# Issuing the later loads of K, Q and V one query tile apart in a fused LSH-attention and MLP kernel

## The chip, the cores and the metric

The kernel runs on one core of a Trainium2 chip. The metric is the device time of one execution in microseconds (us). Engines are named as in the profile: PE (TensorE matmul), PEld (its weight load), DVE (VectorE), ACT (ScalarE), POOL (GpSimd), SP (SyncE, whose queue issues most DMAs here).

## The reference

Attention with a hash mask, then an MLP. B, H, S, D = 4, 8, 768, 64; the MLP goes from 512 to 2048 and back to 512.

```python
q_bits = (einsum('bhsd,dk->bhsk', q, proj) > 0); k_bits = the same of k      # 6 bits
mask = q_bucket[:, :, :, None] == k_bucket[:, :, None, :]
scores = where(mask, D**-0.5 * q @ k^T, -1e9)
attn = exp(scores - max); attn = attn / (sum(attn) + 1e-9)
x = (attn @ v), heads side by side                                            # 3072 x 512
h = x @ w_in; g = where(h > 0, h, exp(min(h, 0)) - 1); out = g @ w_out
```

Everything is fp32 at the reference's precision; the kernel gets it from fp16 matmuls on numbers that are split into a high and a low half.

## The kernel before

**Tiling.** Heads go in pairs, four a batch. A chunk is half a batch's sequence (three columns of 128 rows) for all four pairs. The kernel walks through 8 chunks x 4 pairs x 6 query tiles = 192 query tiles; `G` counts them, and a batch has 48. For one tile, `scores` makes a 128 x 768 block in PSUM (`s` or `so`), DVE copies it with its maximum (`pt`), ACT takes the exponent, ACT and DVE split it into two fp16 halves (`hl`), and a DMA transpose on SP's queue turns it (`PT<-hl`). Four tiles after a pair's last query tile, `attend` multiplies `PT` by V (`av`), and `x<-av` copies the result out. In between, the matmuls of the MLP (`h`, `o`, and ACT's and DVE's work on `U`) of the chunk before are interleaved.

**Preparation.** Each pair needs Q per chunk, and K per batch. `prep_k` and `prep_q` have four steps: `load` (fp32 from HBM to `kst` and `qst`, two buffers each), `scale` (sums of squares on ACT, `natk,kx<-kst` and `nat1q,qx<-qst`, then powers of two on DVE), `split` (fp16 halves `natk`, `nat1q`, `nat2q`, then DMA transposes `K<-natk`, `O<-nat1q`, `O<-nat2q`), and `project` (DVE copies K, `COPY K<-K`; PE makes the hash bits `z`, DVE turns them into `zb`, small DMAs `K<-zb` and `O<-zb` put them under K and Q). `prep_v` loads V (`vf`, seven buffers shared with the split halves `vhl`), sums its squares (`natk,vx<-vf`) and splits it.

**What sets the order.** Pairs after the first four are prepared two at a time. The lists `due` and `vdue` hold each step with the query tile at which the code emits it. For a group whose first pair begins at tile `begin`, `lead` gives the tiles of loads and of sums: `begin` less `PREP[0]` and `PREP[1]`, but no earlier than the last split of the group before, which comes 16 tiles ahead of `begin`. V's steps stand at fixed tiles from the end of the batch before. From tile 30 on, PE follows the code's order. The other engines and SP's queue do not: a scheduler simulates the program and lets an instruction go ahead of earlier ones when its inputs and its buffers are free. Every queue is then strictly in order on the chip. SP's DMAs share eight semaphores in turn, so each also waits for the one eight issues ahead.

**What starts at the loads (before).** The tiles for batch 1's first K group were: all four loads (K, Q, K, Q) at 32, sums at 34, scales at 35, splits at 38 and 44. V's were: four loads at 32, sums at 34 to 37, scale at 41, splits at 43, 49, 54, 59.

Of the kernel before, what the change touches and what calls it, by code (L numbers as in the profile page):

```python
# [10 lines left out]
F32 = mybir.dt.float32  # L11
# [18 lines left out]
OTHER = (3, 3)  # L30
MOE_LAGS = (6, 6, 6)
AV_LAG = 4
PREP = (18, 14, 10, 5)
PREP0 = (100, 12, 12, 6)
W_RATE = 6
W_PRE = 2
# [5 lines left out]
V_AFTER = 0  # L42
W_FREE = 5
VPREP = (-50, 0, 1, 2, 4, 6)

# [19 lines left out]
def lsh_attention_moe(  # L67
# [10 lines left out]
    nc = tc.nc  # L78
    B, H, S, D = q.shape
# [3 lines left out]
    P = 128  # L83
    NC = S // P
    NP = H // 2
    HALF = S // 2
    HC = NC // 2
# [210 lines left out]
    kexs = {}  # L298

    def prep_k(b, ps, sts, sgs):  # L300
        def load():
            with after(0, "first") if b == 0 and "first" in ks[0, 0] else nullcontext():
                for p, st, sg_ in zip(ps, sts, sgs):
                    st["kf"] = stg.tile([P, 2 * NC, D], F32, tag="k", name="kst", bufs=2) if sg_.kf is None else sg_.kf
                    nc.sync.dma_start(
                        st["kf"].rearrange("p (h c) d -> p h (c d)", h=2),
                        k[b, 2 * p : 2 * p + 2].rearrange("h (p c) d -> p h (c d)", c=NC),
                    )

        def scale():  # L310
            w = len(ps)
            mx = small.tile([P, 2], F32, tag="kx", name="kx")[:, :w]
            for n, (st, sg_) in enumerate(zip(sts, sgs)):
                squares(mx[:, n : n + 1], flat(st["kf"]), sg_.k1)
            yield
            if b not in kexs:
                kexs[b] = small.tile([P, NP], F32, tag="ke", name="ke", bufs=2)
            _, sc = powers(mx, w, 4.0, QK_TOP, "k", squares=True, ex=kexs[b][:, ps[0] : ps[0] + w])
            for n, st in enumerate(sts):
                st["ksc"] = sc[:, n : n + 1]  # L320

        def split(st, sg_):
            s, nat = st["ksc"], sg_.k1
            scaled("n_hi", nat[:, :, :D], st["kf"], s)
            rest("n_lo", nat[:, :, D:], st["kf"], s, nat[:, :, :D])
            st["K1"] = okp.tile([P, 2 * NC, P], F16, tag="K1", name="K1", bufs=NP)
            st["K2"] = okp.tile([P, 2 * NC, P], F16, tag="K2", name="K2", bufs=NP)
            st["first"] = nc.sync.dma_start_transpose(st["K1"], flat(nat))

        def project(st):  # L330
            k1, k2 = flat(st["K1"]), flat(st["K2"])
            copied("dup", k2[:D], k1[:D])
            quads = [k1[:, u * HALF : (u + 1) * HALF] for u in range(4)]
            st["done"] = bits(k2, ((0, quads), (1, quads)), HALF, 0)

        return load, scale, split, project

    def prep_q(b, c0, nc_, ps, ksts, sts, sgs):
        def load():
            with after(0, "first") if b == 0 and "first" in ks[0, 0] else nullcontext():  # L340
                for p, st, sg_ in zip(ps, sts, sgs):
                    st["qf"] = stg.tile([P, 2 * HC, D], F32, tag="q", name="qst", bufs=2) if sg_.qf is None else sg_.qf
                    st["qf"] = st["qf"][:, : 2 * nc_, :]
                    nc.sync.dma_start(
                        st["qf"].rearrange("p (h c) d -> p h (c d)", h=2),
                        q[b, 2 * p : 2 * p + 2].rearrange("h (p c) d -> p h (c d)", c=NC)[:, :, c0 * D : (c0 + nc_) * D],
                    )

        def scale():
            w = len(ps)  # L350
            mx = small.tile([P, 2], F32, tag="qx", name="qx")[:, :w]
            for n, (st, sg_) in enumerate(zip(sts, sgs)):
                squares(mx[:, n : n + 1], flat(st["qf"]), sg_.q1[:, : 2 * nc_])
            yield
            ex, sc = powers(mx, w, 4.0, QK_TOP, "q", rows=True, squares=True)
            sg = small.tile([P, 2, 2], F32, tag="sg", name="sg")
            c = D**-0.5 * 2.0 ** (-2 * QK_TOP)
            for x in range(2):
                nc.vector.scalar_tensor_tensor(
                    sg[:, x, :w], ex, c if x == 0 else -c, kexs[b][:, ps[0] : ps[0] + w], ALU.mult, ALU.mult  # L360
                )
            for n, st in enumerate(sts):
                st["qsc"], st["sg"] = sc[:, n : n + 1], sg[:, :, n]

        def split(st, sg_):
            s, nat1, nat2 = st["qsc"], sg_.q1[:, : 2 * nc_, :], sg_.q2[:, : 2 * nc_, :]
            scaled("n_hi", nat1[:, :, :D], st["qf"], s)
            rest("n_lo", nat2[:, :, :D], st["qf"], s, nat1[:, :, :D])
            copied("dup", nat1[:, :, D:], nat1[:, :, :D])
            st["O1"], st["O2"] = o_ring.take(2 * nc_, (b, c0))  # L370
            nc.sync.dma_start_transpose(st["O1"], flat(nat1))
            nc.sync.dma_start_transpose(st["O2"], flat(nat2))

        def project(st):
            w = nc_ * P
            o1, o2 = flat(st["O1"]), flat(st["O2"])
            hi, lo = ([x[:, u * w : (u + 1) * w] for u in range(2)] for x in (o1, o2[:D]))
            st["made"] = bits(o2, ((2, hi), (2, lo), (3, lo)), w, 1)

        return load, scale, split, project  # L380


    def prep_v(b):
        st = {"f": [], "v": [None] * NP}

        def load():
            mx = small.tile([P, NP], F32, tag="vx", name="vx")
            for p in range(NP):
                f = vpool.tile([P, 2, NC, D], F32, tag="v", name="vf")
                with tc.issue_after(ks[b, V_AFTER]["done"].ins) if b == 0 else nullcontext():  # L390
                    nc.sync.dma_start(
                        f.rearrange("p h c d -> p h (c d)"),
                        v[b, 2 * p : 2 * p + 2].rearrange("h (p c) d -> p h (c d)", c=NC),
                    )
                st["f"].append(f)
            st["mx"] = mx
            if b == 0:
                for p in range(NP):
                    sums(p)

        def sums(p):
            f = st["f"][p]
            squares(st["mx"][:, p : p + 1], f.rearrange("p h c d -> p (h c d)"), steady.k1 if b else junk0)

        def top():
            m1 = small.tile([P, 1], F32, tag="vx1", name="vx1")
            with behind_max():
                nc.vector.tensor_reduce(m1, st["mx"], axis=AX.X, op=ALU.max)
            st["m1"] = m1

        def scale():
            with behind_max():
                st["ex"], st["sc"] = powers(st["m1"], 1, 2.0**-34, V_TOP, "v", squares=True)

        def split(p):
            f = st["f"][p]
            t = vpool.tile([P, 2, NC, 2, D], F16, tag="v", name="vhl")
            st["v"][p] = t
            for j in range(2):
                scaled("v_hi", t[:, j, :, 0, :], f[:, j], st["sc"])  # L420
                rest("v_lo", t[:, j, :, 1, :], f[:, j], st["sc"], t[:, j, :, 0, :])

        parts = [lambda p=p: sums(p) for p in range(NP)] if b else []
        return st, [load] + parts + ([top, scale] if b else [lambda: (top(), scale())]) + [lambda p=p: split(p) for p in range(NP)]


    wst = {}
# [284 lines left out]
    def prep(ns):  # L712
# [9 lines left out]
        if c["c0"] == 0:  # L722
            parts.insert(0, (prep_k(b, ps, ksts, sgs), ksts))

        def load():
            for part, _ in parts:
                part[0]()

        made = []

# [15 lines left out]
            part, sts = parts[x]  # L746
            part[3](sts[i])

        return load, sums, scale, split, project, len(parts)


    due = []
# [4 lines left out]
    for ns in groups:  # L757
# [18 lines left out]
            split_at[0] = max(lead[1], split_at[0])  # L776
        else:
            lead[0] = max(lead[0], last["split"])
            lead[1] = max(lead[1], lead[0])
            split_at[0] = max(split_at[0], lead[1], last["project"])  # L780
        steps = prep(ns)
        due += [(lead[0], ns[0], 0, steps[0]), (lead[1], ns[0], 1, steps[1]), (lead[1] + (not early), ns[0], 1.5, steps[2])]
        split_at[0] = max(split_at[0], due[-1][0])
        steps = steps[1:]
        for i, n in enumerate(ns):
# [15 lines left out]
        vs[b] = prep_v(b)  # L801
    for b in range(1, B):
        s0 = [c for c in chunks if c["b"] < b][-1]["end"]
        vdue += [(s0 + x, s) for x, s in zip((-16, -14, -13, -12, -11, -9, -7, -5, 1, 6, 11), vs[b][1])]


    wq = list(wsplits)
# [50 lines left out]
    def weights(n):  # L858
        nonlocal w_credit, w_at
        w_credit += n  # L860
        while w_credit >= 1:

            at = (w_at + (2 if w_at >= NSI else 1)) * SL
            users = {x[1] for x in due} | ({"v"} if len(vdue) == NP + 2 + (B - 1) * (2 * NP + 3) else set())
            if any(a < at + SL and at < z and users & u for a, z, u in guards):
                break
            if w_at not in w64 and w_at < NSI + NSO:
# [109 lines left out]
```

## Time and profile before

| | us |
|---|---|
| median of three runs | 940.16 (939.42 to 942.19) |
| the profiled execution | 942.09 |
| its span, first to last instruction | 940.3 |
| mean granted TensorE clock of the span | 0.955 |
| PE busy | 818.6 |
| DVE busy | 713.6 |
| ACT busy | 706.1 |

The time of an execution is a little longer than the span of its instructions. Rows of the profile below are in us from the span's start. A row of the timeline gives start, length, engine, source line, operation, output and inputs, shape and count; in brackets stands how long the engine was idle before it and what released it. `SPq` rows are DMA issues: their length is how long SP was held by the issue, and not how long the transfer took.

### The profile page before, as it was taken

What the parts mean: (1) busy time and instruction counts of PE and PEld (TensorE: products, weight loads), DVE (VectorE), ACT (ScalarE), POOL (GpSimd) and SP (SyncE); (2) the same over time, 40 slices, a digit from 0 to 9 for tenths busy, and PEclk for the clock granted to TensorE, in tenths of its full rate; (3) what the DMA queues carried; (4) which work ended last, traced back from release to release, by engine and by line L of the source; (5) the groups of instructions that cost most, each with busy time, mean ns of one, the idle gap of its engine ahead of it and who ended that gap; (6) DMA issues with size and microseconds to landing.
All of it is one profiled execution on the core that took longest, in us unless ns stands there. A gap on an engine that the chain in (4) does not pass through costs nothing.

```text
span 940.3 us, 14736 instructions
## 1 busy us (share of the span) xinstructions
PE 818.6 (87%) x4975; PEld 420.0 (45%) x4975; DVE 713.6 (76%) x1625; ACT 706.1 (75%) x1277; POOL 99.3 (11%) x142
## 2 busy tenths in 40 slices
PE   2446655899886999999987999999989999999997
PEld 0113222354443555554544554545545555555553
DVE  6799999898974878788974777788888687775332
ACT  4566786898967878878976877879887788786443
POOL 1000000011111010210010010210121102110000
PEclk9998665899998999999998999999999999999999
DMA  9999987679788767788698658787697767665000
GB/s 275 264 230 211 243 228 165 119 133 173 137 141 165 137 119 136 152 163 177 137 179 148 136 100 143 156 174 139 113 193 129 129 119 153 102 101 101 34 1 35
DMA packets 404924, 138.49 MB, mean 147 GB/s; under 512 B 380976, under 2 KB 399152, under 8 KB 404848
## 3 DMA queue, kind: packets, MB, share of 16 engines
q1 hardware_dynamic: 402864, 131.91, 70.8%
q0 software_dynamic: 1680, 5.51, 1.8%
q8 instruction: 39, 0.64, 0.3%
q14 instruction: 37, 0.30, 0.1%
q10 hardware_dynamic: 304, 0.13, 0.1%
HBM read 35.65 MB, written 6.29 MB: 45 GB/s over the span
## 4 chain that ended last, share of the span: by engine, by line
PE 46%; DVE 9%; ACT 5%; DMA 4%; issue 3%; POOL 1%; SPq 0%; DVEq 0%; ACTq 0%; POOLq 0%
PE o L646 16%; PE h L603 16%; PE s L508 6%; PE av L560 6%; DMA PT<-hl 3%; DVE pt L520 2%; DVE hl L152 2%; ACT pt L536 2%; DMA K<-natk 2%; POOL nb L533 1%; PE z L286 1%; DVE U L626 1%; ACT U L143 1%; ACT hl L143 1%; DVE vhl L152 1%
## 5 line engine op out<-in xcount | busy, mean ns | idle before, releaser
L646 PE MATMUL o<-W,U 128*128 128x512 f16 x1152 | 281.0, 381 | 2.8 <-ACT U L143 2.8
L603 PE MATMUL h<-x,W 128*128 128x384 f16 x1536 | 279.6, 326 | 0.8 <-DVE x L570 0.8
L536 ACT ACTIVATE pt<-pt,nb,sg 128x768 f32<-128x768 f32 x192 | 195.4, 1020 | 64.3 <-POOL nb L533 63.7
L152 DVE SCALAR_TENSOR_TENSOR hl<-pt,r,hl 128x768 f16<-128x768 f32 x192 | 190.7, 1011 | 11.5 <-ACT hl L143 11.4
L603 PEld LDWEIGHTS <-W 128*128 128x128 f16 x1536 | 147.5, 98 | 112.0 <-issue 10.9
L520 DVE TENSOR_SCALAR_CACHE_REDUCE pt<-s 128x768 f32<-128x768 f32 x177 | 168.1, 949 | 38.8 <-DMA PT<-hl 19.4
L143 ACT ACTIVATE hl<-pt,r 128x768 f16<-128x768 f32 x192 | 168.4, 925 | 16.0 <-issue 6.9
L508 PE MATMUL s<-K,O 128*128 128x384 f16 x708 | 153.6, 340 | 22.8 <-DVE pt L520 15.8
L646 PEld LDWEIGHTS <-U 128*128 128x128 f16 x1152 | 111.0, 98 | 124.6 <-issue 6.6
L533 POOL TENSOR_SCALAR nb<-m,sg 128x2 f32<-128x2 f32 x96 | 85.0, 886 | 746.8 <-DVE pt L520 392.5
L560 PE MATMUL av<-PT,vhl 128*64 128x384 f16 x1152 | 115.2, 353 | 24.9 <-DMA PT<-hl 22.3
L152 DVE SCALAR_TENSOR_TENSOR U<-U,sgg 128x384 f16<-128x384 f32 x128 | 78.6, 614 | 69.2 <-ACT U L143 68.3
L508 PEld LDWEIGHTS <-O 76*128 76x128 f16 (+1 forms) x768 | 74.5, 102 | 125.7 <-issue 50.7
L143 ACT ACTIVATE U<-U,sgg 128x384 f16<-128x384 f32 x128 | 77.8, 608 | 56.0 <-DVE U L626 55.8
L560 PEld LDWEIGHTS <-vhl 128*64 128x64 f16 x1152 | 72.3, 118 | 75.6 <-DMA PT<-hl 20.2
L626 DVE SCALAR_TENSOR_TENSOR U<-U 128x384 f32<-128x384 f32 x128 | 70.6, 552 | 37.0 <-ACT U L618 36.8
L616 ACT ACTIVATE U<-h,ch 128x384 f32<-128x384 f32 x128 | 72.6, 567 | 31.3 <-PE h L603 31.2
L618 ACT ACTIVATE U<-h,ch 128x384 f32<-128x384 f32 x128 | 72.8, 568 | 0.0
L472 PE MATMUL acc<-W,ones 128*128 128x512 bf16 x32 | 18.0, 562 | 40.1 <-DVE W L469 39.9
L536 ACT ACTIVATION_READ_ACCUMULATOR pt<-pt,nb,sg 128x1 f32 x192 | 36.3, 189 | 0.0
L570 DVE SCALAR_TENSOR_TENSOR x<-av,x 128x384 f16<-128x384 f32 x32 | 17.7, 554 | 19.3 <-ACT x L569 19.3
L291 DVE TENSOR_SCALAR zb<-z,pjt 64x384 f16<-64x384 f32 (+1 forms) x48 | 29.0, 603 | 0.3 <-PE z L286 0.3
(107 smaller groups left out, 520.5 us busy)
## 6 DMA issues: line engine op xcount, KB each, us to landing
U<-in_moe_w_in_dram SPq DMA_DIRECT2D x12, 512.0 KB
vf<-in_v_dram SPq DMA_DIRECT2D x16, 384.0 KB
U<-in_moe_w_out_dram SPq DMA_DIRECT2D x12, 512.0 KB
qst<-in_q_dram SPq DMA_DIRECT2D x30, 192.0 KB
kst<-in_k_dram SPq DMA_DIRECT2D x14, 384.0 KB
out_dram<-W POOLq DMA_DIRECT2D x14, 256.0 KB, 4.7
PT<-hl SPq DMA_TRANSPOSE x192
W<-in_moe_w_in_dram SPq DMA_DIRECT2D x4, 512.0 KB
```

Source lines behind the costliest of these rows:

```text
L143: nc.scalar.activation(o, x, AF.Copy, scale=s)
L152: nc.vector.scalar_tensor_tensor(o, x, s, hi, ALU.mult, ALU.subtract)
L508: nc.tensor.matmul(s_tile[:, n, :HALF], st[o][:rows, at, :], kst[kk][:rows, j * NC + n * HC : j * NC + (n + 1) * HC, :].rearrange("p a b - ...
L520: top = nc.vector.tensor_scalar(pt.rearrange("p (n e) -> p n e", n=2), s_tile[:, :, :HALF], CLAMP, None, ALU.max, ALU.max, accum_out=duo[0 ...
L533: nc.gpsimd.tensor_scalar(nb[:, :w], m[:, :w], st["sg"][:, 1:2], 1.0, ALU.mult, ALU.mult)
L536: nc.scalar.activation(pt, pt, AF.Exp, bias=nb[:, n : n + 1], scale=st["sg"][:, 0:1], accum_out=sm[:, n : n + 1])
L560: nc.tensor.matmul(av[j * D : (j + 1) * D], vt[:, j, c, vx, :], PTs[j][:, :, px, c, :], start=n == 0, stop=n == last,)
L603: nc.tensor.matmul(h, WH[:, g * KT + t, wx, fc * P : (fc + 1) * P], c["xs"][t][:, xx, :], start=n == 0, stop=n == 3 * KT - 1,)
L616: nc.scalar.activation(e, h, AF.Exp, scale=c["ch"])
L618: nc.scalar.activation(hp, h, AF.Relu, scale=c["ch"])
L626: nc.vector.scalar_tensor_tensor(e, e, -1.0, hp, ALU.add, ALU.min)
L646: nc.tensor.matmul(o[t][:, :DO], g16[:, gx, t * P : (t + 1) * P], WH[:, NSI + 1 + f, wx, :], start=f == 0 and i == 0, stop=f == NF - 1 and ...
```

## The change

`load` of K and Q now takes one pair at a time, `load` of V one pair of heads. In `due` each later group's loads stand one tile apart, from the tile at which all four stood (`PREP[0]` goes from 18 to 21, but the last split of the group before still decides), and the sums come at least three tiles after the first load. V's steps have 14 tiles of their own.

```diff
-PREP = (18, 14, 10, 5)
+PREP = (21, 14, 10, 5)
+VLATER = (-18, -17, -16, -14, -13, -12, -11, -10, -8, -6, -4, 1, 6, 11)
...
     def prep_k(b, ps, sts, sgs):
-        def load():
+        def load(i):
+            p, st, sg_ = ps[i], sts[i], sgs[i]
...
+        loads = [lambda part=part, i=i: part[0](i) for i in range(len(ns)) for part, _ in parts]
...
-            lead[1] = max(lead[1], lead[0])
+            lead[1] = max(lead[1], lead[0] + 3)
...
-        due += [(lead[0], ns[0], 0, steps[0]), (lead[1], ns[0], 1, steps[1]), (lead[1] + (not early), ns[0], 1.5, steps[2])]
+        if early:
+            due.append((lead[0], ns[0], 0, lambda loads=steps[0]: [load() for load in loads]))
+        else:
+            due += [(lead[0] + i, ns[0], 0, load) for i, load in enumerate(steps[0])]
+        due += [(lead[1], ns[0], 1, steps[1]), (lead[1] + (not early), ns[0], 1.5, steps[2])]
...
-        vdue += [(s0 + x, s) for x, s in zip((-16, -14, -13, -12, -11, -9, -7, -5, 1, 6, 11), vs[b][1])]
+        vdue += [(s0 + x, s) for x, s in zip(VLATER, vs[b][1])]
```

For batch 1's first K group this gives K at 32, Q at 33, K at 34, Q at 35, sums at 35, scales at 36, splits still at 38 and 44. V's loads stand at 30, 31, 32 and 34, its sums at 35 to 38, its scale at 42, its splits at 44, 49, 54 and 59.

What the scheduler makes of that is another matter. SP's queue in the middle of batch 2's first chunk (tiles 100 to 106), before; `K_4842<-zb` and `O_4848<-zb` are the copies of hash bits, `kst` holds K of the batch to come:

```order
190 L344 DMA qst<-in_q_dram 128x2x192 x2
191 L391 DMA vf<-in_v_dram 128x2x384
192 L305 DMA kst<-in_k_dram 128x2x384 x2
193 L552 DMA_TRANSPOSE PT<-hl 128x12x128 x2
194 L295 DMA K_4842<-zb 12x384 x4
195 L295 DMA O_4848<-zb 12x384 x2
196 L552 DMA_TRANSPOSE PT<-hl 128x12x128 x4
```

And the same place with the change:

```order
183 L345 DMA qst<-in_q_dram 128x2x192 x2
184 L392 DMA vf<-in_v_dram 128x2x384
185 L555 DMA_TRANSPOSE PT<-hl 128x12x128 x2
186 L296 DMA K_4842<-zb 12x384 x4
187 L296 DMA O_4848<-zb 12x384 x2
188 L306 DMA kst<-in_k_dram 128x2x384 x2
189 L555 DMA_TRANSPOSE PT<-hl 128x12x128 x6
```

The two loads of K, still side by side, have moved from ahead of two transposes of P to behind them and behind six copies of bits. The middle of batch 1's first chunk shows the same move; batch 3's has no K or V to load.

ACT at that place (tiles 104 to 106) before; `natk,kx<-kst` are the sums of K's squares, `natk,vx<-vf` those of V's:

```order
409 L207 ACTIVATE natk,kx<-kst 128x768
410 L207 ACTIVATE nat1q,qx<-qst 128x384
411 L616 ACTIVATE U<-h,ch 128x384
412 L618 ACTIVATE U<-h,ch 128x384
413 L143 ACTIVATE hl<-pt,r 128x768 x2
414 L143 ACTIVATE U<-U,sgg 128x384
415 L207 ACTIVATE natk,kx<-kst 128x768
416 L536 ACTIVATE pt,sm<-pt,nb,sg 128x768 x2
417 L207 ACTIVATE natk,vx<-vf 128x768
418 L569 ACTIVATE x_5232<-av 128x384
419 L207 ACTIVATE natk,vx<-vf 128x768 x2
420 L143 ACTIVATE U<-U,sgg 128x384
```

And with the change:

```order
413 L208 ACTIVATE nat1q,qx<-qst 128x384
414 L619 ACTIVATE U<-h,ch 128x384
415 L621 ACTIVATE U<-h,ch 128x384
416 L144 ACTIVATE hl<-pt,r 128x768 x2
417 L144 ACTIVATE U<-U,sgg 128x384
418 L539 ACTIVATE pt,sm<-pt,nb,sg 128x768 x2
419 L572 ACTIVATE x_5232<-av 128x384
420 L208 ACTIVATE natk,kx<-kst 128x768 x2
421 L144 ACTIVATE U<-U,sgg 128x384
422 L144 ACTIVATE hl<-pt,r 128x768 x2
423 L208 ACTIVATE natk,vx<-vf 128x768
```

K's two sums have moved behind `x<-av`, and V's come later or, for one, earlier.

SP's queue at the start of K's preparation for batch 2 (tiles 84 to 90) before; `K_4221<-natk` is the first transpose of K:

```order
159 L552 DMA_TRANSPOSE PT<-hl 128x12x128 x2
160 L372 DMA_TRANSPOSE O_4228<-nat2q 128x6x128
161 L371 DMA_TRANSPOSE O_4227<-nat1q 128x6x128
162 L344 DMA qst<-in_q_dram 128x2x192
163 L552 DMA_TRANSPOSE PT<-hl 128x12x128 x2
164 L295 DMA O_3914<-zb 12x384 x2
165 L328 DMA_TRANSPOSE K_4221<-natk 128x12x128
166 L305 DMA kst<-in_k_dram 128x2x384
```

And with the change, where K is `K_4220`:

```order
152 L555 DMA_TRANSPOSE PT<-hl 128x12x128 x4
153 L296 DMA O_3919<-zb 12x384 x2
154 L329 DMA_TRANSPOSE K_4220<-natk 128x12x128
155 L372 DMA_TRANSPOSE O_4226<-nat1q 128x6x128
156 L373 DMA_TRANSPOSE O_4227<-nat2q 128x6x128
157 L306 DMA kst<-in_k_dram 128x2x384
158 L345 DMA qst<-in_q_dram 128x2x192
```

K's transpose now comes ahead of Q's two and of the load of Q, where it came behind them.

More of the change, by code (lines that the diff above doesn't have):

```diff
@@ L300, in prep_k @@
     def prep_k(b, ps, sts, sgs):
-        def load():
+        def load(i):
+            p, st, sg_ = ps[i], sts[i], sgs[i]
             with after(0, "first") if b == 0 and "first" in ks[0, 0] else nullcontext():
[L303 to L308, printed above, removed]
+                st["kf"] = stg.tile([P, 2 * NC, D], F32, tag="k", name="kst", bufs=2) if sg_.kf is None else sg_.kf
+                nc.sync.dma_start(
+                    st["kf"].rearrange("p (h c) d -> p h (c d)", h=2),
+                    k[b, 2 * p : 2 * p + 2].rearrange("h (p c) d -> p h (c d)", c=NC),
+                )
         def scale():
@@ L338, in prep_q, with load @@
     def prep_q(b, c0, nc_, ps, ksts, sts, sgs):
-        def load():
+        def load(i):
+            p, st, sg_ = ps[i], sts[i], sgs[i]
             with after(0, "first") if b == 0 and "first" in ks[0, 0] else nullcontext():
[L341 to L347, printed above, removed]
+                st["qf"] = stg.tile([P, 2 * HC, D], F32, tag="q", name="qst", bufs=2) if sg_.qf is None else sg_.qf
+                st["qf"] = st["qf"][:, : 2 * nc_, :]
+                nc.sync.dma_start(
+                    st["qf"].rearrange("p (h c) d -> p h (c d)", h=2),
+                    q[b, 2 * p : 2 * p + 2].rearrange("h (p c) d -> p h (c d)", c=NC)[:, :, c0 * D : (c0 + nc_) * D],
+                )
         def scale():
@@ L384, in prep_v, with load, first @@
         st = {"f": [], "v": [None] * NP}
-        def load():
-            mx = small.tile([P, NP], F32, tag="vx", name="vx")
-            for p in range(NP):
[L389 to L399, printed above, removed]
+        def load(p):
+            if p == 0:
+                st["mx"] = small.tile([P, NP], F32, tag="vx", name="vx")
+            f = vpool.tile([P, 2, NC, D], F32, tag="v", name="vf")
+            with tc.issue_after(ks[b, V_AFTER]["done"].ins) if b == 0 else nullcontext():
+                nc.sync.dma_start(
+                    f.rearrange("p h c d -> p h (c d)"),
+                    v[b, 2 * p : 2 * p + 2].rearrange("h (p c) d -> p h (c d)", c=NC),
+                )
+            st["f"].append(f)
+        def first():
+            for p in range(NP):
+                load(p)
+            for p in range(NP):
+                sums(p)
         def sums(p):
@@ L421, in split @@
                 rest("v_lo", t[:, j, :, 1, :], f[:, j], st["sc"], t[:, j, :, 0, :])
-        parts = [lambda p=p: sums(p) for p in range(NP)] if b else []
-        return st, [load] + parts + ([top, scale] if b else [lambda: (top(), scale())]) + [lambda p=p: split(p) for p in range(NP)]
+        parts = [lambda p=p: load(p) for p in range(NP)] + [lambda p=p: sums(p) for p in range(NP)] if b else [first]
+        return st, parts + ([top, scale] if b else [lambda: (top(), scale())]) + [lambda p=p: split(p) for p in range(NP)]
     wst = {}
@@ L723, in prep @@
             parts.insert(0, (prep_k(b, ps, ksts, sgs), ksts))
-        def load():
-            for part, _ in parts:
-                part[0]()
+        loads = [lambda part=part, i=i: part[0](i) for i in range(len(ns)) for part, _ in parts]
         made = []
@@ L747, in project @@
             part[3](sts[i])
-        return load, sums, scale, split, project, len(parts)
+        return loads, sums, scale, split, project, len(parts)
     due = []
@@ L863, in weights @@
             at = (w_at + (2 if w_at >= NSI else 1)) * SL
-            users = {x[1] for x in due} | ({"v"} if len(vdue) == NP + 2 + (B - 1) * (2 * NP + 3) else set())
+            users = {x[1] for x in due} | ({"v"} if len(vdue) == NP + 2 + (B - 1) * len(VLATER) else set())
             if any(a < at + SL and at < z and users & u for a, z, u in guards):
```

## The prediction

> **What bounds the kernel now.** I read the page first: busy times, slices, and the chain that ended last.
>
> ```profile
> PE 818.6 (87%) x4975; PEld 420.0 (45%) x4975; DVE 713.6 (76%) x1625; ACT 706.1 (75%) x1277; POOL 99.3 (11%) x142
> PE   2446655899886999999987999999989999999997
> PEclk9998665899998999999998999999999999999999
> DMA  9999987679788767788698658787697767665000
> PE 46%; DVE 9%; ACT 5%; DMA 4%; issue 3%; POOL 1%; SPq 0%; DVEq 0%; ACTq 0%; POOLq 0%
> ```
>
> TensorE (PE) leads, with dents in the slices at 270 to 300, 495 and 700 us. Busy time by stage comes next, one chunk of 24 query tiles a row (start:end, length, then each engine's busy time, granted clock, DMA share, GB/s):
>
> ```profile
> 201.80:316.40 114.60, 99.48 (x624) 51.22 (x620) 90.44 (x204) 94.92 (x174) 16.63 (x15) 0.97 0.81 151
> 316.40:412.20 95.80, 95.80 (x619) 51.23 (x619) 74.15 (x169) 76.87 (x142) 12.11 (x15) 1.00 0.75 137
> 412.20:520.70 108.50, 98.95 (x627) 51.59 (x625) 84.12 (x193) 89.07 (x165) 13.01 (x15) 0.97 0.83 160
> 520.70:618.00 97.30, 95.58 (x618) 50.71 (x611) 74.08 (x169) 76.93 (x141) 11.68 (x16) 1.00 0.71 135
> 618.00:719.40 101.40, 95.83 (x627) 50.16 (x624) 84.16 (x193) 84.40 (x155) 14.69 (x15) 1.00 0.80 150
> 719.40:814.10 94.70, 94.70 (x614) 50.25 (x606) 73.62 (x156) 75.31 (x134) 11.60 (x16) 1.00 0.70 131
> ```
>
> Rows 2, 4 and 6 are bound by PE at about 95 us. Rows 1, 3 and 5 hold a change of batch (I call them batch starts 1, 2 and 3) and take 114.6, 108.5 and 101.4. What can be won lies in these, and what is won stays won, since PE has no slack behind them to lose it in. TensorE's rows there (start, length, what it is; in brackets the idle time before it and its releaser):
>
> ```profile
> 239.47 3.11 PE L560 MATMUL av<-PT,vhl 128*64 128x384 f16 x35 [1.76 <-DMA PT<-hl]
> ...
> 299.70 5.04 PE L560 MATMUL av<-PT,vhl 128*64 128x384 f16 x35 [7.30 <-DMA PT<-hl]
> ...
> 502.78 5.88 PE L560 MATMUL av<-PT,vhl 128*64 128x384 f16 x35 [4.82 <-DMA PT<-hl]
> ...
> 704.23 3.11 PE L560 MATMUL av<-PT,vhl 128*64 128x384 f16 x35 [1.52 <-DMA PT<-hl]
> ```
>
> The same product, in the same place of three batches, waits 7.30, 4.82 and 1.52 us for a transpose of P, and takes 5.04 and 5.88 us where the wait was long, 3.11 where it was short. SP's queue just ahead tells the batches apart (length: how long SP was held by the issue):
>
> ```profile
> 283.39 1.09 SPq L344 DMA_DIRECT2D qst<-in_q_dram  x2
> 284.52 0.47 SPq L391 DMA_DIRECT2D vf<-in_v_dram  x1
> 285.03 0.99 SPq L305 DMA_DIRECT2D kst<-in_k_dram  x2
> 286.12 10.77 SPq L552 DMA_TRANSPOSE PT<-hl  x2
> ...
> 490.01 0.98 SPq L305 DMA_DIRECT2D kst<-in_k_dram  x2
> 491.08 9.70 SPq L552 DMA_TRANSPOSE PT<-hl  x2
> ...
> 504.00 1.48 SPq L295 DMA_DIRECT2D O<-zb  x2
> ...
> 693.64 1.08 SPq L344 DMA_DIRECT2D qst<-in_q_dram  x2
> 694.95 5.47 SPq L552 DMA_TRANSPOSE PT<-hl  x2
> ```
>
> At 283 and 488 us two loads of Q, one of V and two of K (the next batch's, issued some 25 tiles early because their buffers are free) stand ahead of the two transposes; at 693, with no batch left, only Q's. The transposes then hold SP for 10.77, 9.70 and 5.47 us: the DMA engines are full. The stretches around them (length, PE, PEld, DVE, ACT, POOL, clock, DMA share, GB/s):
>
> ```profile
> 286.00:292.00 6.00, 6.00 (x35) 2.73 (x33) 4.27 (x10) 6.00 (x16) 1.80 (x3) 1.00 1.01 282
> ...
> 300.00:305.00 5.00, 5.00 (x37) 2.76 (x34) 1.93 (x3) 3.18 (x7) 0.60 (x1) 0.64 0.04 9
> ...
> 503.00:508.00 5.00, 5.00 (x34) 2.76 (x31) 1.94 (x3) 2.96 (x6) 0.61 (x1) 0.50 0.04 9
> ```
>
> DMA is at a share of 1.01 while TensorE is about to starve, and at 0.04 just after; the clock is 0.64 and 0.50 after the two long waits.
>
> **The change, part by part.** No instruction is added or taken away on the chip; the 64 loads of K, Q and V stay as they are. What moves is the order on the queues, and not as the numbers say: K's loads still go out in pairs. In both batch starts 1 and 2 the pair now stands behind the two transposes of P and the six small copies of sign bits, whose last ended at 504.00 + 1.48 = 505.5 in batch start 2. That is the stretch where the DMA share was 0.04.
>
> *Term 1, the transposes no longer wait for K.* Two loads are 2 x 384 KB = 786 KB; at the 282 GB/s of the row they take 2.8 us. Other bounds: the hold on SP beyond batch start 3's is 10.77 - 5.47 = 5.3 and 9.70 - 5.47 = 4.2 for V and two K, of which K is two thirds, 3.5 and 2.8; from the issue of the transposes to the product's start it is 13.6, 11.7 and 9.3 us, so V and K cost 4.3 and 2.4, K's share 2.9 and 1.6. I take 2.8 in each place, ends 1.6 and 3.5. Term 1 is -5.6. Waits left: 7.30 - 2.8 = 4.5 and 4.82 - 2.8 = 2.0.
>
> *Term 2, the clock.* The product takes 3.11 us at full clock; the slow one costs 5.88 - 3.11 = 2.8 in batch start 2, 5.04 - 3.11 = 1.9 in batch start 1. Which wait drops the clock:
>
> ```profile
> 178.38 4.02 PE L646 MATMUL o<-W,U 128*128 128x512 f16 x9 [2.85 <-ACT U L143]
> ...
> 273.41 0.81 PE L508 MATMUL s<-K,O 128*128 128x384 f16 x4 [2.10 <-DVE pt L520]
> ...
> 177.00:184.00 7.00, 5.62 (x15) 2.12 (x16) 6.25 (x11) 6.18 (x11) 0.00 (x0) 0.53 0.61 112
> ```
>
> A wait of 2.85 had a clock of 0.53 around it, one of 2.10 none (the stage's slice stands at 9). So 2.0 is nearest to a wait that costs nothing, and 4.5 to the 4.82 that did drop it: batch start 2 gains 2.8, batch start 1 nothing. Term 2 is -2.8, ends 0 and -4.7. The Trainium skill, "TensorE: Matmul & The Clock Gate" (Part 1: The HAM clock gate), says that the clock halves after at least one idle window of some 3.4 us, and that these windows run free. By that rule, a wait of 4.5 mostly straddles two windows without filling one, the 1.9 of batch start 1 would come off too, and the sum would be 1.9 lower; the trace does not bear the rule out strictly, as its 2.85 was enough.
>
> *Term 3, K's transposes.* At batch starts 2 and 3 VectorE (DVE) stood for K's transpose, which made PE wait for scores; SP's queue ahead of the first ran as the upper rows show:
>
> ```profile
> 411.07 1.21 SPq L372 DMA_TRANSPOSE O<-nat2q  x1
> ...
> 413.67 0.57 SPq L344 DMA_DIRECT2D qst<-in_q_dram  x1
> ...
> 419.88 1.46 SPq L328 DMA_TRANSPOSE K<-natk  x1
> ...
> 425.17 0.55 DVE L162 COPY K<-K 64x1536 f16<-64x1536 f16 x1 [3.84 <-DMA K<-natk]
> ...
> 629.16 0.55 DVE L162 COPY K<-K 64x1536 f16<-64x1536 f16 x1 [2.08 <-DMA K<-natk]
> ...
> 428.58 0.81 PE L508 MATMUL s<-K,O 128*128 128x384 f16 x4 [1.67 <-DVE pt L520]
> ...
> 634.09 0.81 PE L508 MATMUL s<-K,O 128*128 128x384 f16 x4 [1.76 <-DVE pt L520]
> ```
>
> Now Q's two transposes and a load of Q come behind K's, 411.07 to 414.24 or 3.2 us of SP. K may land up to 3.2 earlier, but its input is also scaled about a tile later. Between 0 and -3.4 (both PE waits), I take half, -1.7.
>
> *Term 4, given back.* In batch start 1 one more transpose or load of Q stands ahead of P's in two places, and PE already waits 1.76 there (239.47): 192 KB at 282 GB/s is 0.7; I take +0.9 with the slip around it. The scales of K, Q and V come a tile later, but their splits keep their tile, so nothing is charged (ends 0 and one tile, 95 / 24 = 4 us). Before 120 us, loads of Q, Q and K, 768 KB, now stand together ahead of weights that two of them stood behind: the same bytes in the same stretch, 0, ends +-2.8 (786 KB at the same rate). For K's late arrival on ScalarE (ACT), see the rivals: +1.0.
>
> Sum: -5.6 - 2.8 - 1.7 + 0.9 + 1.0 = -8.2. The profiled execution took 942.09 (span 940.3), 1.93 above the median of 940.16; so 933.9 for it and 932 as a median.
>
> **Rivals.**
>
> *Late K on ACT (slower).* Before, ACT's sums of K's squares stood thus:
>
> ```profile
> 496.01 0.84 ACT L207 ACTIVATE natk<-kst 128x768 bf16<-128x768 f32 x1 [1.76 <-DMA kst<-in_k_dram]
> ```
>
> From issue at 490.01 to use it took 6.0 us, and ACT stood 1.76 for it. Now both sums stand right behind x<-av and ahead of the P splits and the MLP's tiles, and K is issued after 505.5 - 2.8 = 502.7. ACT gets there soon after the product ends, near 500.0 + 3.1 = 503.1; K lands between 502.7 + 1.0 + 2.8 = 506.5 and 502.7 + 6.0 = 508.7. ACT waits 3 to 5 us, with TensorE two PSUM banks ahead; I charged 1.0 for the two places. If all of a 6.0 us arrival and of two sums (2 x 0.84) reaches TensorE in both places, that is +15.4, less 9.2 of gain: 948.3 in this execution, 946 as a median. It decides above 4.6 us a place. For it: an in-order engine with a wait at its head. Against: a full MLP tile is in hand, and before, ACT carried three sums of V's squares at the same spot. The Trainium skill, "DMA: Bandwidth & Descriptors" (Rules for kernel authors), says to issue a DMA early and wait for it late; by that rule this part of the change points the wrong way.
>
> *The loads were not what the transposes waited for (same).* V, Q and three output stores still stand ahead. If these fill the gap, the wait shrinks by the lower 1.6 or less a place and both clock drops stay: -3.2 + 1.9 of term 4, about 939.
>
> *Both waits fall clear of the drop (faster still).* Batch start 1's wait of 3.8 to 4.5 lies between the 2.85 and the 4.82 that dropped the clock, which speaks against it; what speaks for it is that neither tells where in the clock's own rhythm a wait began. With K at 3.5 a place, term 2 at -4.7 and term 3 at -3.4: -15.1 + 1.9, so 927 as a median. The rule of the page on the clock gate, above, would make this the likelier of the two.
>
> **How the numbers follow.** Forecast 0.50, clear of both drops 0.17, same 0.19, slower 0.14. The forecast alone spans 927 to 937. Both ends are taken out to the rivals: 922 (every term at its end, startup's -2.8 with it) to 942. About 0.3% (2.8 us) is what a measurement can tell from no change, so faster means under 937.3, slower over 943.0; a little of the same rival falls below. Chances: 0.70, 0.17, 0.13.
>
> **What would show it.** Right: the product near 299 and 499 us waits under 5 and under 3 us, and runs at 3.1 us in batch start 2; SP's hold by the two transposes is about 8 and 7 us; K's pair goes out where DMA was idle. Wrong: ACT rows natk<-kst with waits over 4.6 us and TensorE's tiles h waiting for ACT; a long wait unchanged with V alone ahead; or a later start of the chunk at 201.8 us.

## The result, and the profile after

The changed kernel took 932.72 us (median; 931.26 to 937.61), the kernel before 941.06 beside it; the ratio of the mean times is 0.9923, 95% interval 0.9895 to 0.995. Repeated on the chip of the last experiments it was 935.62 against 939.76: 0.9962 (0.9941 to 0.9984). By these ratios the change is faster by 4 to 7 us. The forecast of 932 and the sign were right; how the time came about was not as forecast, and the second measurement says that the sum was on the high side.

From the page of the changed kernel: busy times, then PE's and the clock's slices (compare with those of before):

```profile
PE 817.0 (87%) x4975; PEld 419.0 (45%) x4975; DVE 714.0 (76%) x1625; ACT 705.8 (76%) x1277; POOL 97.3 (10%) x142
PE   2437664889889999999998999999989999999997
PEclk9999665999999999999999999999999999999999
```

Busy times are the same; the dents at 270 to 300 and at 500 us are shallower. Busy time by stage, the three stages with a batch start:

```profile
202.50:312.00 109.50, 99.40 (x632) 51.15 (x630) 87.99 (x199) 92.81 (x173) 13.02 (x16) 0.98 0.81 157
...
408.30:511.90 103.60, 98.77 (x634) 52.62 (x633) 83.22 (x192) 88.09 (x166) 12.57 (x15) 0.98 0.84 166
...
610.40:712.80 102.40, 98.12 (x630) 50.99 (x629) 84.28 (x193) 85.39 (x157) 13.36 (x15) 0.98 0.81 148
```

114.6, 108.5 and 101.4 became 109.5, 103.6 and 102.4: batch start 1 won 5.1, batch start 2 4.9, batch start 3 lost 1.0. The three stages between took 1.9 more in all. SP's queue at batch starts 1 and 2:

```profile
285.17 6.22 SPq L555 DMA_TRANSPOSE PT<-hl  x2
291.44 3.48 SPq L296 DMA_DIRECT2D K<-zb  x4
295.04 1.78 SPq L296 DMA_DIRECT2D O<-zb  x2
296.86 1.02 SPq L306 DMA_DIRECT2D kst<-in_k_dram  x2
...
485.07 6.64 SPq L555 DMA_TRANSPOSE PT<-hl  x2
```

K's pair went out at 296.86, behind the transposes, and these held SP for 6.22 and 6.64 us in place of 10.77 and 9.70. TensorE's rows at the same four places, and two waits for scores that the kernel before did not have:

```profile
240.05 3.11 PE L563 MATMUL av<-PT,vhl 128*64 128x384 f16 x35 [2.21 <-DMA PT<-hl]
294.16 4.69 PE L563 MATMUL av<-PT,vhl 128*64 128x384 f16 x35 [2.29 <-DMA PT<-hl]
327.81 0.81 PE L511 MATMUL s<-K,O 128*128 128x384 f16 x4 [1.61 <-DVE pt L523]
494.46 4.76 PE L563 MATMUL av<-PT,vhl 128*64 128x384 f16 x35 [3.28 <-DMA PT<-hl]
528.33 0.81 PE L511 MATMUL s<-K,O 128*128 128x384 f16 x4 [1.75 <-DVE pt L523]
695.64 4.79 PE L563 MATMUL av<-PT,vhl 128*64 128x384 f16 x35 [2.56 <-DMA PT<-hl]
```

The two long waits shrank from 7.30 and 4.82 to 2.29 and 3.28. All three products now run at half clock for a part (4.7 to 4.8 us in place of 3.11), and in batch start 3 the wait grew from 1.52 to 2.56.

This table gathers the same place from all profiles: at each batch start the wait for the transposes and the length of the product behind it (its 35 or 36 matmuls take 3.1 us at full clock), then the time. The kernels named are those of the experiments below; ratios are to the kernel before on the same chip.

| kernel | start 1 | start 2 | start 3 | median us | ratio (95%) |
|---|---|---|---|---|---|
| before | 7.30, 5.04 | 4.82, 5.88 | 1.52, 3.11 | 941.06 | 1 |
| the change | 2.29, 4.69 | 3.28, 4.76 | 2.56, 4.79 | 932.72 | 0.9923 (0.9895–0.995) |
| change_again | 4.67, 5.93 | 3.99, 4.43 | 3.06, 5.90 | 935.62 | 0.9962 (0.9941–0.9984) |
| spread_only | 5.19, 5.07 | 4.05, 4.79 | 1.01, 3.11 | 937.70 | 0.9972 (0.9954–0.999) |
| sums_later_only | 4.20, 4.79 | 3.38, 5.79 | 2.68, 4.79 | 935.14 | 0.9942 (0.9918–0.9966) |
| term1_alone | 2.33, 4.70 | 2.89, 4.72 | 1.16, 3.11 | 939.78 | 0.9991 (0.9975–1.0006) |
| term3_alone | 6.44, 5.40 | 4.56, 4.51 | 1.28, 3.11 | 938.67 | 0.9989 (0.9974–1.0004) |
| k_groups_later | 3.42, 3.11 | 3.53, 4.76 | 0.93, 3.11 | 933.75 | 0.9962 (0.994–0.9983) |
| q_groups_later | 5.84, 5.82 | 5.25, 5.52 | 1.03, 3.11 | 940.40 | 1.0034 (1.001–1.0058) |
| all_loads_behind | 2.10, 4.67 | 1.64, 3.09 | 1.33, 3.08 | 931.27 | 0.9935 (0.9905–0.9965) |
| stores_behind_too | 0, 3.12 | 0, 3.12 | 0, 3.12 | 929.23 | 0.9913 (0.9882–0.9944) |
| stores_behind_alone | 0, 3.24 | 0.70, 3.11 | 0, 3.12 | 930.94 | 0.992 (0.9894–0.9947) |
| stores_k_v_behind | 0, 3.12 | 0, 3.12 | 0, 3.23 | 928.76 | 0.9876 (0.9847–0.9905) |
| stores_loads_again | 0, 3.12 | 0, 3.12 | 0, 3.12 | 929.77 | 0.9897 (0.9872–0.9923) |

### The profile page after: what moved, and what is told of

It reads as the page before. It is cut to its first block, busy times and chain, and to the rows that moved or that the text cites. A ratio compares the mean times of both kernels' runs of the same rounds, so it can differ in the third digit from the quotient of the medians.

```text
span 934.1 us, 14712 instructions
## 1 busy us (share of the span) xinstructions
PE 817.0 (87%) x4975; PEld 419.0 (45%) x4975; DVE 714.0 (76%) x1625; ACT 705.8 (76%) x1277; POOL 97.3 (10%) x142
## 5 line engine op out<-in xcount | busy, mean ns | idle before, releaser
L536 POOL TENSOR_SCALAR nb<-m,sg 128x2 f32<-128x2 f32 x96 | 83.1, 866 | 740.3 <-DVE pt L523 478.6
L287 PE MATMUL z<-O,pjz 64*32 64x384 f16 (+1 forms) x192 | 27.0, 358 | 3.6 <-DVE x L573 1.4
```

Of the source, the lines that this page charges most:

```text
L536: nc.gpsimd.tensor_scalar(nb[:, :w], m[:, :w], st["sg"][:, 1:2], 1.0, ALU.mult, ALU.mult)
```

## The experiments

**Which part of the change does it.** The change has two parts that can be had apart: loads one by one, and sums a tile later. spread_only, against the change, keeps the loads apart (the last two of a group share a tile) and puts the sums back:

```diff
-VLATER = (-18, -17, -16, -14, -13, -12, -11, -10, -8, -6, -4, 1, 6, 11)
+VLATER = (-18, -17, -16, -14, -14, -13, -12, -11, -9, -7, -5, 1, 6, 11)
-            lead[1] = max(lead[1], lead[0] + 3)
+            lead[1] = max(lead[1], lead[0] + 0)
-            due += [(lead[0] + i, ns[0], 0, load) for i, load in enumerate(steps[0])]
+            due += [(lead[0] + min(i, 2), ns[0], 0, load) for i, load in enumerate(steps[0])]
```

sums_later_only keeps the later sums and puts the loads back:

```diff
-VLATER = (-18, -17, -16, -14, -13, -12, -11, -10, -8, -6, -4, 1, 6, 11)
+VLATER = (-16, -16, -16, -16, -13, -12, -11, -10, -8, -6, -4, 1, 6, 11)
-        if early:
+        if early or not False:
             due.append((lead[0], ns[0], 0, lambda loads=steps[0]: [load() for load in loads]))
```

> The loads one by one, the sums, scales and splits at the tiles of before. Theory A (the time comes from what stands ahead of what on SP's queue and DVE's, and the later sums brought that): K's pair stays ahead of the two transposes of P in batch starts 1 and 2, K's transposes stay behind Q's; same as before, ratio 0.998 to 1.002, waits near 300 and 503 us still about 7 and 5 us. Theory B (loads issued a tile apart disturb the transposes less): about 0.992, 934 us, both waits shorter by 2 us or more.

> The loads all at once as before, the sums, scales and first splits at the later tiles of the change. Theory A: K's pair goes behind the two transposes of P in both places and K's transposes ahead of Q's in batch starts 2 and 3, as in the change: 0.992 (0.989 to 0.995), 933 us. Theory B: 1.000, 940 us.

The loads alone gave 0.9972, the later sums alone 0.9942. With the loads alone K's pair stays ahead of the transposes. SP's queue and the product at batch start 1 of spread_only:

```profile
285.83 0.98 SPq L306 DMA_DIRECT2D kst<-in_k_dram  x2
286.91 8.35 SPq L555 DMA_TRANSPOSE PT<-hl  x2
...
297.24 5.07 PE L563 MATMUL av<-PT,vhl 128*64 128x384 f16 x35 [5.19 <-DMA PT<-hl]
```

Theory A has the larger part right by the middle values: -5.4 us with the later sums, which change the order, and -2.6 with the loads alone, for which it expected 0.998 to 1.002. The two intervals overlap (0.9918 to 0.9966 and 0.9954 to 0.999), so that the sums bring most of it is likely, not shown. Of theory B's shorter waits the first came (5.19 for 7.30), the second hardly (4.05 for 4.82). In that profile the hold by the two transposes is 8.35 us, where the same order at this place held 10.77 in before, 9.54 in term3_alone and 9.85 in q_groups_later. Whether this is the rhythm of one execution or what V's sums, which stand elsewhere on ACT, do to it, was not settled.

**Terms 1 and 3 by themselves**, on the kernel before. `issue_after` queues an instruction behind another on its queue and waits for nothing; `pts_` lists the transposes of P in order of emission. First K's loads behind P's transposes (term1_alone), then Q's transposes behind K's (term3_alone):

```diff
-            with after(0, "first") if b == 0 and "first" in ks[0, 0] else nullcontext():
+            with after(0, "first") if b == 0 and "first" in ks[0, 0] else (tc.issue_after(pts_[48 * b - 43].ins) if b > 1 and p < 2 else nullcontext()):
```

```diff
-            nc.sync.dma_start_transpose(st["O1"], flat(nat1))
-            nc.sync.dma_start_transpose(st["O2"], flat(nat2))
+            with tc.issue_after(ksts[sts.index(st)]["first"].ins) if c0 == 0 and b > 1 else nullcontext():
+                nc.sync.dma_start_transpose(st["O1"], flat(nat1))
+                nc.sync.dma_start_transpose(st["O2"], flat(nat2))
```

> The kernel before with one edit: the four loads of K for pairs 0 and 1 of the last two batches are queued behind the two transposes of P that they stood ahead of. The prediction's terms 1 and 2 with their price (-5.6 - 2.8 + 1.0 = -7.4): 0.992, 933 us. As the trace of the changed kernel reads (2.1 us won at batch start 1, none at batch start 2): -2, 0.998, 938 us. If these loads are not what the transposes waited for: 1.000. In the trace SP's hold by the two transposes falls from 10.8 and 9.7 to 6 or 7 us under the first two, and stays above 9 under the third.

> The kernel before with one edit: in the last two batches each pair's transposes of Q are queued behind its first transpose of K. The prediction's term 3: -1.7, 0.998, 938 us. As the trace of the changed kernel reads (3.9 us won between tiles 78 and 102, 2.9 between 126 and 150): -6.8, 0.993, 933 us. DVE's waits for K's transposes near 425 and 629 us (3.84 and 2.08) go below 1 us under both; they differ in whether PE's gain is larger than its waits for scores there (1.67 and 1.76).

Term 1 by itself did at the place what the prediction said, and did not make the kernel faster: 0.9991. TensorE's rows of term1_alone, with SP's row on Q's transpose in time order:

```profile
295.13 4.70 PE L565 MATMUL av<-PT,vhl 128*64 128x384 f16 x35 [2.33 <-DMA PT<-hl]
324.06 3.09 PE L565 MATMUL av<-PT,vhl 128*64 128x384 f16 x35 [2.34 <-DMA PT<-hl]
324.51 1.23 SPq L373 DMA_TRANSPOSE O<-nat1q  x1
499.85 4.72 PE L565 MATMUL av<-PT,vhl 128*64 128x384 f16 x35 [2.89 <-DMA PT<-hl]
533.71 0.81 PE L512 MATMUL s<-K,O 128*128 128x384 f16 x4 [1.48 <-DVE pt L524]
```

The waits fell by 7.30 - 2.33 = 5.0 and 4.82 - 2.89 = 1.9. Behind them stand new ones that before did not have, 2.34 at 324 and 1.48 at 534. By the starts of DVE's copies of scores (term1_alone less before, at tiles 51, 57, 66, 84): -1.3, -6.1, -1.5, -0.7. What was won between tiles 51 and 57 was gone by tile 66. The rows of ACT and SP behind the place say where:

```profile
299.87 0.49 ACT L574 ACTIVATE x<-av 128x384 f16<-128x384 f32 x1 [3.23 <-PE av L565]
300.82 0.84 ACT L209 ACTIVATE natk<-kst 128x768 bf16<-128x768 f32 x1 [0.46 <-DMA kst<-in_k_dram]
302.84 0.84 ACT L209 ACTIVATE natk<-kst 128x768 bf16<-128x768 f32 x1 [1.09 <-DMA kst<-in_k_dram]
305.15 1.75 ACT L144 ACTIVATE hl<-pt,r 128x768 f16<-128x768 f32 x2
317.09 3.29 SPq L556 DMA_TRANSPOSE PT<-hl  x2
```

Before, both sums of K stood ahead of `x<-av`, the second of them (294.58) while TensorE waited; now they stand behind it, and ACT waits 0.46 and 1.09 for the late K. ACT comes to `x<-av` 4.9 us earlier than before (299.87 for 304.77), to the next splits of P only 2.5 earlier (305.15 for 307.69), and the next product's last transposes go out 0.8 us earlier (317.09 for 317.89). So TensorE, which is 4 us early, waits there. SP's queue is not full there: between 296 and 325 us SP itself waited 5.0 and 3.0 us for results of DVE. This is read from the rows; no run takes K's sums on ACT apart from the late K.

Term 3 by itself gave 0.9989, -1.0 us; its interval holds both the -1.7 charged and nothing. DVE's wait for the first K in batch start 2's chunk went from 3.84 to 2.68, PE's for scores from 1.67 to 0.72; in batch start 3's a second wait came for it (DVE 2.08 became 1.36 and 1.55). Below 1 us, as expected, it did not go.

**Where the change gives back.** In the trace of the changed kernel ACT stands for Q's one staging buffer just before the new wait for scores at 327.81:

```profile
324.48 0.61 ACT L144 ACTIVATE nat1q<-qst,qs 128x384 f16<-128x384 f32 x1 [1.16 <-DMA O<-nat1q]
```

Q's transposes, two transposes of P later on SP than before, free that buffer late. So the tile shift was taken apart by groups: k_groups_later keeps it for groups with K alone, q_groups_later (with the loads as in spread_only) for those without.

```diff
-            lead[1] = max(lead[1], lead[0] + 3)
+            lead[1] = max(lead[1], lead[0] + (3 if chunks[pairs[ns[0]][0]]["c0"] == 0 else 0))
```

```diff
-            lead[1] = max(lead[1], lead[0] + 3)
+            lead[1] = max(lead[1], lead[0] + (2 if chunks[pairs[ns[0]][0]]["c0"] == 0 else 3))
-            due += [(lead[0] + i, ns[0], 0, load) for i, load in enumerate(steps[0])]
+            due += [(lead[0] + min(i, 2), ns[0], 0, load) for i, load in enumerate(steps[0])]
```

> The changed kernel, but groups that load only Q keep their sums, scales at the tiles of before; groups with K stay as changed. Theory (give-back): in the changed kernel TensorE has new waits near 328 and 352 us (1.61, 0.61) and near 528 and 552 us (1.75, 0.61), because the later sums of Q's groups push O<-nat1q and O<-nat2q behind two more transposes of P, and the one staging buffer of Q is free only after them. Here these two transposes go ahead of them again: the waits go, 4.6 us, ratio to before 0.987 (0.984 to 0.990), 928 us. Rival: the transposes of Q take from those of P what they give, and PE waits for PT instead: 0.992.

> The other half: only the groups that load Q alone have sums and scales a tile later; groups with K have theirs as before; V as changed; loads one by one. K's pair stays ahead of the two transposes of P. Theory (give-back): the waits near 300 and 503 us stay as before (5 to 7 and 4 to 5 us), the new ones near 328 and 528 us come: 1.002 to 1.004, 942 us. Rival (Q's later sums cost nothing): 0.997 to 1.000 like the loads one by one alone.

With K's groups alone the waits at 328 and 528 went, but others came in the next product, much as the rival said, of 1.71 us (put down to the copies of sign bits) and, at 520.72, of 0.87 for P's transposes:

```profile
294.55 3.11 PE L563 MATMUL av<-PT,vhl 128*64 128x384 f16 x35 [3.42 <-DMA PT<-hl]
320.70 3.08 PE L563 MATMUL av<-PT,vhl 128*64 128x384 f16 x35 [1.71 <-DMA K<-zb]
493.86 4.76 PE L563 MATMUL av<-PT,vhl 128*64 128x384 f16 x35 [3.53 <-DMA PT<-hl]
```

0.9962 is no better than the change's 0.9923 and 0.9962. Q's groups alone were slower, 1.0034, with both long waits much as before; the new waits near 328 and 528 did not come there. So the gain hangs on K's groups, and the theory on Q's buffer named a wait that is there in the change, but not one whose removal pays.

**What the transposes still wait for.** Queued behind the two transposes of P, at the three batch starts: first all loads (with K's groups alone later), then the three output stores of 256 KB too, taken from POOL's queue to SP's; then the stores alone, on the changed kernel; then the stores with V's and K's loads, Q's staying ahead.

```diff
-            (nc.sync if final else nc.gpsimd).dma_start(rows, ot)
+            if c["c0"] == 0 and c["b"] < B - 1:
+                with tc.issue_after(pts_[min(48 * c["b"] + 53, len(pts_) - 1)].ins):
+                    nc.sync.dma_start(rows, ot)
+            else:
+                (nc.sync if final else nc.gpsimd).dma_start(rows, ot)
```

The loads get `tc.issue_after` in the same way.

> K's groups later as above, and in the three batch starts the two loads of Q, that of V and the pair of K are all queued behind the two transposes of P. Theory (bytes ahead of the transposes): Q's two and V's one are 786 KB, 2.8 us at the row's 282 GB/s; the waits near 294 and 494 us fall from 2.3 and 3.3 to below 1, the clock stays at full there, and each place gains 2.3 + 1.6: some 6 to 8 us more than with K's groups later alone, 0.980, 921 us. Rival 1 (the transposes are bound by their own packets and by the three output stores): the waits stay above 1.5 us and the gain is under 2 us. Rival 2 (K comes too late): ACT waits for kst over 3 us and TensorE for scores, slower than K's groups later alone.

> As the one before, and the three output stores of 256 KB that POOL issues just then go out on SP's queue behind the two transposes of P, in the three batch starts. Theory (bytes): 786 KB less beside the transposes, waits near 294 and 494 us at zero: 1 to 3 us under the one before. Rival (SP becomes the bound): the copies of sign bits and the next transposes of P stand behind the stores' issue, and the waits move to z or to the next product: no better, or slower by 1 to 3 us.

> The changed kernel once more, on the chip of the three below, so that they can be set against it: 0.992 (0.989 to 0.995) if its gain does not hang on the chip; a second profile shows how far its waits near 294, 494 and 695 us (2.29, 3.28, 2.56) and the slow products behind them repeat. If the half clock follows the length of the wait alone, waits over 2 us are followed by a product of 4.7 us again; if it follows the clock's own rhythm too, some will be followed by 3.1 us.

> The changed kernel with one edit: the three output stores of the three batch starts go out on SP's queue behind the two transposes of P, in place of POOL's queue beside them. If the stores are what the transposes still wait for: the three waits go from 2.29, 3.28, 2.56 to below 0.5 and the three products run at 3.1 us, -7 to -12 against the changed kernel, 923 to 927 us. If the loads of Q and V that stay ahead are (384 and 384 KB): waits stay above 2 us, under 1 us won. If TensorE only waits elsewhere for it (for scores, behind ACT or SP): waits for PT go and the time falls by less than 4 us.

> As the last of the four runs before (stores, V's and K's loads behind the two transposes of P, K's groups alone later), but Q's two loads stay ahead of them. There ACT stood 3.63 us for Q and 1.96 for V, and TensorE 3.93 for scores near 305 us. Theory (late loads held ACT): ACT's wait for Q goes, TensorE's 3.93 and 2.90 fall below 2, and the time is 2 to 4 us under that run's, about 926 us. Rival (Q's 384 KB are as much in the way of the transposes): waits of 1 to 2 us for PT come back in the three places and the time is the same or up to 3 us longer.

> The last of the four runs before once more (all loads and the stores behind the two transposes of P, K's groups alone later), on the same chip as the changed kernel. If its 929 us were not the chip's doing: 3 to 6 us under the changed kernel. If they were: within 2 us of it.

With no load ahead the waits were still 2.10, 1.64 and 1.33, and the gain over k_groups_later was 2.5 us, not 6 to 8: the bytes of the loads were not what was left, near to what rival 1 said (waits above 1.5, gain under 2). With the stores behind, the waits are gone but for one of 0.70, in every kernel that has it, and all products run at 3.1 to 3.2 us. One edit on the changed kernel thus took away waits of 4.67, 3.99 and 3.06 and some 6.9 us of slow matmuls (products of 5.93, 4.43 and 5.90 against 3.1), by the profile of change_again. That profile is of the longest of its twelve executions (940.58), and the execution profiled here took 929.30, so 11.3 of these 18 us show in the time; between the medians it is 935.62 - 930.94 = 4.7 us, less than the 7 to 12 expected. The rows of ACT and PE in stores_behind_alone say where the rest stayed:

```profile
299.96 0.84 ACT L209 ACTIVATE natk<-kst 128x768 bf16<-128x768 f32 x1 [4.09 <-DMA kst<-in_k_dram]
...
304.21 0.81 PE L512 MATMUL s<-K,O 128*128 128x384 f16 x4 [3.00 <-DVE pt L524]
...
504.00 1.03 PE L512 MATMUL s<-K,O 128*128 128x384 f16 x4 [3.40 <-DVE pt L524]
```

This is the prediction's slower rival, late K on ACT: 4.09 us of wait at the head of an in-order engine, and 3.00 us of it reach TensorE. In the changed kernel the same K is as late (issued at 296.86, here at 296.36), but TensorE stands for P then, ACT stands for the product until 298.89, and its waits for K are 0.56 and 1.15. The wait for P was the cover of the late K. With V's sums ahead of K's and Q on time (stores_k_v_behind), it is split into smaller ones:

```profile
298.01 0.84 ACT L209 ACTIVATE natk<-vf 128x768 bf16<-128x768 f32 x1 [2.50 <-DMA vf<-in_v_dram]
...
303.14 0.84 ACT L209 ACTIVATE natk<-kst 128x768 bf16<-128x768 f32 x1 [2.04 <-DMA kst<-in_k_dram]
...
305.63 0.81 PE L512 MATMUL s<-K,O 128*128 128x384 f16 x4 [0.83 <-DVE pt L524]
310.95 0.81 PE L512 MATMUL s<-K,O 128*128 128x384 f16 x4 [1.36 <-DVE pt L524]
```

That is the fastest version by its median, 928.76 us, 0.9876 of before and 6.9 us under the changed kernel on the same chip. It was expected 2 to 4 us under the kernel of stores_loads_again and was 1.0 under it, which their intervals do not tell apart; TensorE's waits for scores did fall, from 4.42 and 3.06 there to parts of 0.2 to 1.4, but a wait of 2.37 for the sign bits of Q stands new at 321.44. stores_loads_again was 5.9 us under the changed kernel, so the gain is not the chip's doing.

The edit on the stores does two things: it moves 768 KB from beside the transposes to behind them, and it takes the stores from POOL's queue to SP's. No run does one without the other. POOL's own time is no rival: in the changed kernel POOL issued the last of the three at 287.55 and stood idle for 4.73 us before its next work.

## Why the prediction was right or wrong

**Term 1 (-5.6).** The mechanism is right: K's pair went behind the transposes, SP's hold fell to 6.22 and 6.64 (8 and 7 were said) and the two waits by 5.0 and 1.5. In the second profile they fell by 2.6 and 0.8, with holds of 7.67 and 7.39. The mis-sized step is that a wait's gain was carried to the end. "What is won stays won, since PE has no slack behind them to lose it in" was the sentence, and term1_alone refutes it: it cut the same waits by 6.9 in all, and the kernel was 0.9 us faster, not clear of none. PE has no slack there, but the wait had covered work of ACT: with K behind the transposes, ACT waits 1.5 us for it and sums its squares behind the product, the next transposes are 0.8 us earlier, and TensorE waits 2.34 us more at the next product. Terms 1 and 3 by themselves made 0.9 + 1.0 = 1.9 us, the later sums together 5.4. What the sums bring besides was not taken apart; in the changed kernel one sum of V fewer stands ahead of ACT's next two splits of P, and these come 4.3 and 3.7 us earlier than before (303.38 and 311.07), in term1_alone 2.5 and 1.4.

**Term 2 (-2.8).** Wrong. The step was "2.0 is nearest to a wait that costs nothing". Batch start 2 kept 3.28 of its wait and its product took 4.76; batch start 3, which was not in the sum, waited 2.56 and lost its full clock too. Over all profiles the length of the wait does not decide it alone: 2.10 (all_loads_behind), 2.29 and 2.33 were followed by 4.7 us, 3.42 (k_groups_later) by 3.11. What decides is how much of the wait falls into one window of a fixed grid of 3.41 us (last section). The wait of 2.10 at 273.41, from which the step was drawn, lay across an edge of that grid, at 272.93; where the 2.0 that was forecast would lie on it could not be known.

**Term 3 (-1.7).** By itself -1.0 (interval -2.4 to +0.4), in line with the charge but not clear of none. In the changed kernel six waits for scores of before, 8.22 us from 428 to 691 us, became 0.59 and 0.61, but with 0.80 twice for `x` and 1.75 + 0.61 + 0.46 + 0.57 new between 528 and 588 us: a larger removal and a larger return than the term had.

**Term 4 (+1.9).** The 0.9 at 239 us measured 2.21 - 1.76 = 0.45. The 1.0 for the late K: ACT's waits for it were 0.56, 1.15 and 1.40. What was given back came elsewhere, at Q's transposes (1.61 and 1.75 above) and in batch start 3. There, by the starts of DVE's copies, the kernel went from -8.6 to -10.2 against before between tiles 147 and 150; TensorE then waited 1.0 longer for the same transposes and lost 1.7 to the clock, and the kernel stood at -6.9 by tile 156.

**Rivals.** Late K on ACT did not decide in the changed kernel. What the runs show for it is not the MLP tile in hand, as argued, but that TensorE waits for P at the same time; without that wait it costs 3.0 and 3.4, and in term1_alone it is part of what was given back. "The loads were not what the transposes waited for" was half true: K's pair did hold them, but the three stores, named in that rival and not priced, held what was left. Behind all loads they took waits of 2.10, 1.64 and 1.33 to zero and 2.0 us of time, and 4.7 us on the changed kernel; V's and Q's loads took 3.42 and 3.53 to 2.10 and 1.64, and 2.5 us. "Both waits clear of the drop" did not occur.

So the total came out near the forecast with term 1 near its size at the place (6.5 and 3.4 us of waits in the two profiles, for 5.6) and partly given back, term 2 missing, and removals and returns at scores that nearly cancel. It held in part by luck: the second measurement, -3.6 by its ratio (0.0038 x 940), lies 4.6 above the -8.2.

## What to carry to other kernels

Price a wait that is taken away only as far as the next place where the same engine waits: ask what work of other engines the wait covered, and whether the engine that arrives earlier only waits longer there. When DMA is full while an engine starves, list everything in flight by bytes and queue, the stores on another engine's queue too; here, with all loads moved away, three stores still held the transposes. A late transfer that costs nothing may be covered by the very wait that the next edit removes.

## What the runs showed of the hardware

TensorE's clock fell after idle times of 2.10, 2.29 and 2.33 us and stayed up after one of 3.42; over the stretch 294.5 to 299 of the changed kernel the granted clock was 0.68, over 294.5 to 298 of k_groups_later 1.00:

```profile
294.50:299.00 4.50, 4.50 (x37) 2.59 (x34) 0.54 (x2) 1.48 (x5) 0.00 (x0) 0.68 0.25 68
...
294.50:298.00 3.50, 3.45 (x38) 2.23 (x39) 0.00 (x0) 0.71 (x3) 0.00 (x0) 1.00 0.40 121
```

In each of the fourteen traces the half-clock spells begin and end on a grid of 3.41 us (those after 40 us and before 900). Cut along it, the same places read thus, two windows of the changed kernel, then three of k_groups_later (length, then PE busy; the clock is the third number from the end):

```profile
290.58:293.99 3.41, 1.29 (x6) 0.38 (x4) 2.35 (x5) 3.30 (x6) 0.88 (x1) 1.00 0.94 199
293.99:297.41 3.42, 3.25 (x22) 1.88 (x24) 1.05 (x2) 1.88 (x4) 0.00 (x0) 0.50 0.07 16
...
289.38:292.79 3.41, 1.75 (x8) 0.60 (x6) 2.67 (x5) 3.41 (x8) 0.26 (x1) 1.00 1.17 196
292.79:296.21 3.42, 1.66 (x22) 1.17 (x24) 1.28 (x2) 2.12 (x5) 0.00 (x0) 1.00 0.20 56
296.21:299.62 3.41, 3.41 (x28) 1.83 (x25) 1.40 (x4) 1.43 (x3) 0.00 (x0) 1.00 0.72 197
```

The wait of 2.29 left TensorE idle for 2.12 us of one window, and the next ran at half clock; the wait of 3.42 was split into 1.66 and 1.76 us, and none did. Over the fourteen traces, counting TensorE's idle time from its rows, from 200 to 880 us, all 27 full-clock windows with 2.0 us idle or more were followed by half clock, none of the 2700 with under 1.75 us, and 6 of the 16 between.

The Trainium skill, "TensorE: Matmul & The Clock Gate" (Part 1: The HAM clock gate), says that the clock halves after at least one idle window of some 3.4 us and that the window runs free. The free running agrees with 3.42 without a drop; that 2.10 is enough does not agree with a whole idle window. By the counts above it is enough that rather more than half of a window is idle.

The same two transposes in the same order held SP for 10.77, 9.54 and 8.35 us in three kernels, and the wait behind them was 7.30, 6.44 and 5.19. In the changed kernel it was 2.29 in one execution and 4.67 in another. A term taken from one profile of such a place has an uncertainty of some 2 us.
